# Threshold searches of a capacity router: seven rounds of 17 thresholds, or six of 32

## The chip, the cores and the metric

One core of a Trainium2 chip runs the whole program. The metric is its time on the device in microseconds, from a median of several runs. TensorE (PE) multiplies matrices, VectorE (DVE) and ScalarE (ACT) work on elements, GpSimd (POOL) and SyncE (SP) mostly issue transfers here.

## The reference

The program computes attention (8 batches, 8 heads, 576 positions, heads of 64; half of the heads see a local band, half a stride) and then a mixture of 8 experts over its 4608 tokens. The routing goes through all pairs of token and expert in the order of their logits and gives each expert at most 576 tokens:

```python
cap = N // E
logits = x @ w_gate
order = np.argsort(-logits.flatten())
for idx in order:
    tok, e = (int(idx) // E, int(idx) % E)
    if assigned[tok] >= 0 or counts[e] >= cap:
        continue
    assigned[tok] = e
    counts[e] += 1
for e in range(E):
    mask = assigned == e
    out[mask] = np.maximum(x[mask] @ w1[e], 0.0) @ w2[e]
```

## The kernel before, in words

**Stages.** Until about 226 us the kernel does the attention, writes the tokens to a scratch tensor in DRAM and forms the logits `L` (128 partitions x 36 columns x 8 experts). Then it routes and multiplies expert after expert. "Expert k" is the k-th one that fills up, 0 to 7, which is not its index in the weights. Its FFN is two layers of matmuls (`hidden`, L1150, and the second half of `ffn`, L1169).

**A search (L816).** Which expert fills up next, and at which logit, is found by a search on thresholds. Each token points to its best open expert (`rm` its logit, `ohc` a one-hot row). A round compares all 36 columns of 128 tokens with `J1` thresholds (`cm`, L824, on VectorE), counts the tokens above each threshold per expert on TensorE (L840), folds the counts (`red` L843, `r` L846, a matmul L849), marks the thresholds at which an expert has its 576 tokens (`g`, L856), counts the marks by a matmul (L859) and forms the next, finer thresholds (`cand`, L862). With J1 thresholds a round narrows the interval by J1 + 1. `R1` rounds bring 2^25 steps down to 1 and the last round to 1/16 (L96 to L102). Four of the 36 columns (`GC`) go into one counting matmul, so its stationary operand has GC x J1 columns and a round has 9 of them. Expert 0 has a search of its own (`search0`, 6 rounds of 32 thresholds, L768), and expert 7 takes what is left (`rest`). So there are six searches of this kind.

**After a search.** `number` (L880) gives the expert's index `ei`. `weights` (L978) reads it on SP and loads w1 and w2 (8 transfers of 512 KB) into one buffer each, sums their squares on ScalarE (`jk`, L1002), gets a scale (L1008 to L1011) and cuts each weight into a high and a low fp16 part (`w1h`/`w2h` on ScalarE, L1020; `w1l`/`w2l` on VectorE, L1021), 16 cuts to an expert. `slots` and `indices` (L890, L937) work out which tokens the expert has (`rv` and `ohl` on VectorE, then 36 matmuls, L963), `tokens` (L1066) gathers them with five indirect transfers from POOL and turns them with five transposing transfers from SP (L1075). `close` and `take` strike the expert and its tokens out, and the next search begins.

**What sets the order.** TensorE's order is written by the kernel (ScalarE's too, for expert 0); the other engines' orders come from a scheduler with priorities, where the routing's instructions are marked urgent. The writing is done by a planner at the end of the kernel. It goes through the matmuls of an FFN, adds their nominal time to a `clock`, and steps every chain of side work whose due time has come. A search is such a chain: it waits T_COUNT (2950) before the counting matmuls, T_SUM (1350) before L849 and T_STEP (1225) before L859; in expert 1's search these are multiplied by PACE1 (0.55, L813). Side work itself adds nothing to the clock. Two rules bind the chains to the FFNs: expert ph is numbered only when FFN ph - 2 has been written in full (L1128), and cuts that are not yet written when an expert's FFN begins are written there at once (`rush`, L747 to L751). An FFN's hidden tile is read by ScalarE (`hh`, L1166) and VectorE (`hl`, L1167); three such tiles exist in PSUM.

Of the kernel before, what the change touches and what calls it, by code (L numbers as in the profile page):

```python
# [35 lines left out]
VW = D + 1  # L36
NEG = -8.0e9
BIG = 1.0e30
J1, R1, GC = 17, 7, 4
J0, JL, R0, CUTS0 = 32, 16, 6, (16, 12, 8)  # L40
TP = 128
NC = N // TP
# [1288 lines left out]
```

## Time and profile before

| | |
|---|---|
| three runs | 722.44, 726.11, 727.01 us (median 726.11) |
| the profiled execution | 723.2 us, its span 721.4 us |
| mean granted TensorE clock | 0.893 of full speed |
| attention and logits | to about 226 us |
| expert 0's routing | 226 to about 256 us |
| eight FFNs with the routing of experts 1 to 7 beside them | 256 to about 710 us |
| comparisons of the six searches (L824) | 42, 33.3 us of VectorE |
| DMA traffic | 111 MB, of it 64 transfers of 512 KB for the weights |

In the lines below, a timeline row gives the start in us, the duration in us, engine, source line, operation, and the output tile, an arrow, and its inputs; `x9` merges nine in a row, and the brackets hold the idle time of the engine before it and what ended it. A row by windows gives from:to, the length and, for each engine, busy us with the count of instructions, then the granted clock, the DMA share and GB/s. A row of waits gives total us, times, longest. A row of groups gives busy us and mean ns of one, then the engine's idle time before them.

### The profile page before, as it was taken

To read this page: it belongs to the slowest core of one execution; us is meant where nothing else is said; L and a number is where in the kernel's file an instruction comes from. 1 tells how busy PE (TensorE), PEld (TensorE's weight loads), DVE (VectorE), ACT (ScalarE), POOL (GpSimd) and SP (SyncE) were. 2 spreads that over 40 slices of the span, in tenths; PEclk is the share of its full clock that TensorE was granted. 3 is DMA by queue.
4 is the path that set the end of the run, shared out by engine and by line. 5 is a ranking of instruction groups with operands and counts; after the bars stand their busy time and mean duration, and the time that the engine had idled before them with its cause. 6 is when DMAs were issued, how large, how long until landed. Compare 5 with 4: busy or idle time off the path is not lost.

```text
span 721.4 us, 19211 instructions
## 1 busy us (share of the span) xinstructions
PE 625.3 (87%) x8040; PEld 402.7 (56%) x8043; DVE 455.9 (63%) x1368; ACT 320.8 (44%) x497; POOL 153.7 (21%) x152
## 2 busy tenths in 40 slices
PE   6986978889993479999989998989989998699993
PEld 3664756566663346557537646646644744555741
DVE  4786666786876777867657767757666573662200
ACT  3634634653520156473454364274184265753210
POOL 2053323332330020140040040041041023202011
PEclk9667787985885589999999999999999999899998
DMA  9999999999651360680680491392196079551010
GB/s 248 263 256 221 248 262 260 232 247 214 113 134 50 122 200 1 218 213 2 223 194 15 146 254 33 105 265 63 35 295 103 1 271 262 182 96 52 1 38 29
DMA packets 111401, 111.21 MB, mean 154 GB/s; under 512 B 76332, under 2 KB 84102, under 8 KB 110803
## 3 DMA queue, kind: packets, MB, share of 16 engines
q1 hardware_dynamic: 103235, 88.44, 47.7%
q0 software_dynamic: 7360, 21.15, 9.9%
q8 instruction: 63, 1.03, 0.6%
q10 hardware_dynamic: 720, 0.39, 0.2%
q14 instruction: 23, 0.19, 0.1%
HBM read 73.59 MB, written 18.87 MB: 128 GB/s over the span
## 4 chain that ended last, share of the span: by engine, by line
PE 29%; issue 16%; DVE 7%; DMA 6%; ACT 3%; SPq 3%; POOL 2%; another core or an unknown queue 1%; POOLq 0%; ACTq 0%
PE ph L1159 16%; PE ph L1207 9%; DMA w<-in_w_dram 4%; SPq L1075 2%; DVE w2l L1021 2%; ACT jk L1002 2%; DMA xg<-x_scr,idx 2%; POOL out_dram L1218 1%; DVE w1l L1021 1%; DVE hl L1167 1%; PE ph L1201 1%; POOL xg L1072 1%; SPq L987 1%; PE ph L1060 0%
## 5 line engine op out<-in xcount | busy, mean ns | idle before, releaser
L1159 PE MATMUL ph<-xt,w1h 128*128 128x288 f16 (+2 forms) x1024 | 180.0, 288 | 7.0 <-DMA xt<-xg 4.4
L1218 POOL DMA_INDIRECT out_dram<-y,idx x40 | 43.5, 1087 | 351.3 <-ACT y L1217 324.8
L1159 PEld LDWEIGHTS <-w1h 128*128 128x128 f16 x1024 | 97.1, 98 | 34.5 <-issue 6.7
L1159 PE MATMUL ph<-xt,w1l 128*128 128x288 f16 (+2 forms) x512 | 113.3, 288 | 0.0
L1002 ACT ACTIVATE jk<-w 128x1024 f16<-128x1024 f32 x64 | 67.5, 1055 | 73.2 <-DMA w<-in_w_dram 69.3
L1207 PE MATMUL ph<-w2l,hh 128*128 128x512 f16 x256 | 97.9, 382 | 0.0
L1207 PE MATMUL ph<-w2h,hh 128*128 128x512 f16 x256 | 97.7, 382 | 0.0
L1207 PE MATMUL ph<-w2h,hl 128*128 128x512 f16 x256 | 97.7, 382 | 0.0
L1166 ACT ACTIVATE hh<-ph 128x576 f16<-128x576 f32 (+2 forms) x72 | 42.8, 595 | 120.2 <-PE ph L1159 119.2
L1207 PEld LDWEIGHTS <-hh 128*128 128x128 f16 x512 | 48.7, 98 | 58.0 <-issue 9.5
L1167 DVE SCALAR_TENSOR_TENSOR hl<-ph,hh 128x576 f16<-128x576 f32 (+2 forms) x72 | 49.5, 688 | 43.7 <-ACT hh L1166 43.4
L380 ACT ACTIVATE pr<-spa 128x576 f32<-128x576 f32 x32 | 20.8, 650 | 93.9 <-PE spa L376 89.4
L1159 PEld LDWEIGHTS <-w1l 128*128 128x128 f16 x512 | 49.9, 98 | 12.6 <-issue 0.6
L397 PE MATMUL po<-v_s,pr 64*54 64x65 f32 (+1 forms) x768 | 45.6, 276 | 10.2 <-issue 6.5
L428 POOL TENSOR_TENSOR xos<-xs,xos 118x768 f16<-118x768 f32 x16 | 27.2, 1701 | 119.8 <-ACT xos L427 87.8
L1217 ACT ACTIVATE y<-ph,so 128x512 f32<-128x512 f32 x32 | 21.9, 684 | 67.7 <-PE ph L1207 48.1
L1072 POOL DMA_INDIRECT xg<-x_scr,idx x40 | 40.5, 1012 | 50.2 <-issue 34.7
L1021 DVE SCALAR_TENSOR_TENSOR w1l<-w,w_sw,w1h 128x512 f16<-128x512 f32 x64 | 45.7, 745 | 8.0 <-issue 4.6
L1021 DVE SCALAR_TENSOR_TENSOR w2l<-w,w_sw,w2h 128x512 f16<-128x512 f32 x64 | 45.7, 742 | 7.9 <-ACT y L1217 6.8
L397 PEld LDWEIGHTS po<-v_s,pr 64*54 64x54 f32 (+1 forms) x768 | 34.7, 162 | 17.2 <-issue 11.7
L1207 PEld LDWEIGHTS <-hl 128*128 128x128 f16 x256 | 25.1, 98 | 33.2 <-issue 8.1
L1020 ACT ACTIVATE w1h<-w,w_sw 128x512 f16<-128x512 f32 x64 | 41.8, 710 | 3.9 <-DVE ss_e L203 1.8
(613 smaller groups left out, 961.9 us busy)
## 6 DMA issues: line engine op xcount, KB each, us to landing
w<-in_w_dram SPq DMA_DIRECT2D x64, 512.0 KB
kl<-in_kl_dram SPq DMA_DIRECT2D x16, 304.0 KB
v_s<-in_ns_dram SPq DMA_DIRECT2D x16, 292.5 KB
v_l<-in_nl_dram SPq DMA_DIRECT2D x16, 292.5 KB
ks<-in_ks_dram SPq DMA_DIRECT2D x16, 288.0 KB
qs<-in_qt_dram SPq DMA_DIRECT2D x16, 288.0 KB
ql<-in_qt_dram SPq DMA_DIRECT2D x16, 288.0 KB
x_scr<-xol SPq DMA_DIRECT2D x8, 512.0 KB
```

Source lines behind the costliest of these rows:

```text
L397: nc.tensor.matmul(po[r:r + n, j - j0], pr[k, o:o + n], u.vn[k, t, 2 * p + h], start=(j == j0), stop=(j == j1 - 1), skip_group_check=True)
L428: eng.tensor_tensor(u.xo[:nr, :, 1, c], xf, u.xo[:nr, :, 0, c], op=OP.subtract)
L1002: nc.scalar.activation(jk, wf[:, c * n4:(c + 1) * n4].rearrange("p c f -> p (c f)"), AF.Square, scale=1.41422, accum_out=sq[:, c:c + 1])
L1020: nc.scalar.activation(hi[:, c, f], wf[:, c, f], AF.Copy, scale=s_)
L1021: nc.vector.scalar_tensor_tensor(lo[:, c, f], wf[:, c, f], s_, hi[:, c, f], op0=OP.mult, op1=OP.subtract)
L1072: nc.gpsimd.indirect_dma_start(out=xg[:n], out_offset=None, in_=x_rows, in_offset=bass.IndirectOffsetOnAxis(ap=idx[:n, t:t + 1], axis=0))
L1159: nc.tensor.matmul(tile_[:, j, :w], wt[:, d, f * 128:(f + 1) * 128], xt[:, d // 2, xx, d % 2, c], start=(k == 0), stop=(k == 3 * DC - 1))
L1166: nc.scalar.activation(hv, src, AF.Relu)
L1167: nc.vector.scalar_tensor_tensor(lv, src, 0.0, hv, op0=OP.max, op1=OP.subtract)
L1207: nc.tensor.matmul(py, a[:, f, ts_], w[:, f], start=(k == 0), stop=(k == len(todo) - 1))
L1217: nc.scalar.activation(y, py, AF.Copy, scale=so[:, t:t + 1])
L1218: st = nc.gpsimd.indirect_dma_start(out=out_rows, out_offset=bass.IndirectOffsetOnAxis(ap=idx[:n, t:t + 1], axis=0), in_=y[:n], in_offset= ...
```

## The change

```diff
-J1, R1, GC = 17, 7, 4
+J1, R1, GC = 32, 6, 4
```

A round compares with 32 thresholds and narrows the interval by 33, and there are 6 rounds: the widths go 2^25, 1016802, 30813, 934, 29, 1 and then 1/16. `cm` grows from 36 x 17 = 612 to 36 x 32 = 1152 elements a partition. The stationary operand of the counting matmul grows from 4 x 17 = 68 to 128 columns, the counts in PSUM from 68 to 128 partitions. `fold`, `steps` (R1 x (J1 + 2), 133 to 204 elements), `small` and `cand` (18 to 33 elements) grow with them. Nothing else is edited.

Since the planner steps a search by rounds, each search takes one round less on its clock and all that follows it is written earlier, until the rule on FFN ph - 2 holds it. Three places show this.

On VectorE at the start of FFN 6, the order before has expert 6's last cuts (`w2l`) around expert 7's slots (`inc`, `off`, `slot`, `si`; pr__8903 is expert 7's prefix count):

```order
L1190 TENSOR_SCALAR so<-idx,s_8827 128x5
L1021 SCALAR_TENSOR_TENSOR w2l<-w_8477,w_sw_8483,w2h 128x512 x5
L1167 SCALAR_TENSOR_TENSOR hl<-ph,hh 128x576
L913 SCALAR_TENSOR_TENSOR inc<-ones_f,pr__8903 128x72
L915 TENSOR_TENSOR off<-off,pr__8903 128x72
L1021 SCALAR_TENSOR_TENSOR w2l<-w_8477,w_sw_8483,w2h 128x512
L916 TENSOR_TENSOR off<-off,inc 128x72
L1021 SCALAR_TENSOR_TENSOR w2l<-w_8477,w_sw_8483,w2h 128x512
L918 TENSOR_TENSOR slot<-off 128x36
L1021 SCALAR_TENSOR_TENSOR w2l<-w_8477,w_sw_8483,w2h 128x512
L941 CAST si<-slot 128x36
L1167 SCALAR_TENSOR_TENSOR hl<-ph,hh 128x576
```

The order of the change at the same place (pr__8751 is the prefix count, the tail tile `y` belongs to FFN 5):

```order
L1021 SCALAR_TENSOR_TENSOR w2l<-w_8124,w_sw_8130,w2h 128x512 x3
L1215 SCALAR_TENSOR_TENSOR y<-ph,so,yl 64x512
L1021 SCALAR_TENSOR_TENSOR w2l<-w_8124,w_sw_8130,w2h 128x512 x5
L1008 TENSOR_REDUCE ss<-sq 128x1
L1167 SCALAR_TENSOR_TENSOR hl<-ph,hh 128x576
L913 SCALAR_TENSOR_TENSOR inc<-ones_f,pr__8751 128x72
L915 TENSOR_TENSOR off<-off,pr__8751 128x72
L916 TENSOR_TENSOR off<-off,inc 128x72
L918 TENSOR_TENSOR slot<-off 128x36
L941 CAST si<-slot 128x36
```

The eight cuts have moved into the second layer of FFN 5, and the slots follow one another.

On ScalarE at the same place before, the first sum of squares of expert 7 (`jk` from w_8847) stands between output tiles of FFN 5, ahead of expert 6's w2 cuts (from w_8477):

```order
L1217 ACTIVATE y<-ph,so 128x512
L1002 ACTIVATE jk,sq<-w_8847 128x1024
L1217 ACTIVATE y<-ph,so 128x512
L1020 ACTIVATE w2h<-w_8477,w_sw_8483 128x512 x5
L1166 ACTIVATE hh<-ph 128x576
L1020 ACTIVATE w2h<-w_8477,w_sw_8483 128x512 x3
```

In the change expert 7's squares (from w_8695) stand at the end of FFN 5's first layer, and expert 6's w2 cuts (from w_8124) after them, in its second:

```order
L1166 ACTIVATE hh<-ph 128x576
L1002 ACTIVATE jk,sq<-w_8695 128x1024
L1166 ACTIVATE hh<-ph 128x576
L1002 ACTIVATE jk,sq<-w_8695 128x1024 x3
L1217 ACTIVATE y<-ph,so 128x512
L1020 ACTIVATE w2h<-w_8124,w_sw_8130 128x512 x3
L1214 ACTIVATE yl<-ph,so 64x512
```

The squares have moved ahead by most of an FFN.

On VectorE after expert 4's search, the order before runs through slots, the next search's first comparison (`cm`) and the indices without an FFN instruction between them, because this falls into the second layer of FFN 3:

```order
L935 TENSOR_TENSOR L<-L,pen 128x288
L824 TENSOR_TENSOR cm<-rmn,cand_3712 128x612
L942 TENSOR_SCALAR si<-si 128x36
L943 TENSOR_SCALAR si<-si 128x36
L945 CAST sh<-si 128x72
L947 TENSOR_TENSOR ohh<-sh,iota 128x324
L955 TENSOR_TENSOR ohl_7080<-sh,iota 128x768
L949 TENSOR_TENSOR rv_3713<-ohh,val 128x972
```

In the change the same work falls into the first layer of FFN 3, where every hidden tile has its `hl`:

```order
L935 TENSOR_TENSOR L<-L,pen 128x288
L824 TENSOR_TENSOR cm<-rmn,cand_3712 128x1152
L1167 SCALAR_TENSOR_TENSOR hl<-ph,hh 128x576
L942 TENSOR_SCALAR si<-si 128x36
L943 TENSOR_SCALAR si<-si 128x36
L945 CAST sh<-si 128x72
L947 TENSOR_TENSOR ohh<-sh,iota 128x324
L955 TENSOR_TENSOR ohl_6820<-sh,iota 128x768
L949 TENSOR_TENSOR rv_3713<-ohh,val 128x972
L1167 SCALAR_TENSOR_TENSOR hl<-ph,hh 128x576
```

The `hl` of the running FFN now stand between the comparison, `rv` and the second `ohl`.

## The prediction

> **What bounds the kernel now.** The page's first lines say how much work there is, the stages say who sets the pace. "Expert k" is the k-th expert that is routed, 0 to 7; its FFN is its two layers of matmuls.
>
> ```profile
> span 721.4 us, 19211 instructions
> PE 625.3 (87%) x8040; PEld 402.7 (56%) x8043; DVE 455.9 (63%) x1368; ACT 320.8 (44%) x497; POOL 153.7 (21%) x152
> core 0: us, PE busy (x) PEld busy (x) DVE busy (x) ACT busy (x) POOL busy (x), PEclk, DMA share, GB/s
> 256.00:305.00 49.00, 43.92 (x397) 28.72 (x396) 39.85 (x133) 27.49 (x51) 3.03 (x5) 0.97 0.40 123
> 305.00:360.00 55.00, 54.66 (x434) 33.15 (x435) 38.28 (x121) 27.82 (x46) 10.70 (x10) 1.00 0.49 150
> 592.00:650.00 58.00, 49.79 (x352) 30.50 (x351) 31.21 (x71) 36.76 (x64) 14.20 (x15) 0.94 0.68 180
> ```
>
> Everything that the change touches lies after 256 us. There TensorE is the bound: 54.66 of 55 us busy in a good stretch. VectorE is at 38.28 of 55, so on the average it has room. The routing of a later expert runs beside the FFN of an earlier one, and TensorE takes its instructions in a written order, so a search hurts in two ways: by its own matmuls, and wherever one of them stands at the head of TensorE's queue before VectorE is done. The waits of TensorE from 256 to 650 us, longest first, are the second kind.
>
> ```profile
> PE pr__8971 L963 <- DVE rv L949: 5.4, 1, 5.4
> PE ph L1159 <- DMA xt<-xg: 4.4, 4, 1.6
> PE pr__8005 L849 <- DVE r L846: 3.5, 1, 3.5
> PE pr__5752 L849 <- DVE r L846: 3.2, 1, 3.2
> PE pr__7254 L859 <- DVE g L856: 1.1, 1, 1.1
> PE pr__7185 L1010 <- DVE p L966: 1.1, 1, 1.1
> PE pr__7429 L849 <- DVE r L846: 0.8, 1, 0.8
> PE pr__4649 L840 <- DVE cm L824: 0.4, 1, 0.4
> ```
>
> Of all 42 rounds only one made TensorE wait for its comparison (cm, 0.4 us). So the searches are not waited for directly; their end decides when an expert's tokens and weights come.
>
> **The change part by part.** *Rounds removed.* Six searches (experts 1 to 6) lose one round each. What a round costs TensorE is read from the starts around its three pieces.
>
> ```profile
> 330.06 0.41 PE L1159 MATMUL ph<-xt,w1l 128*128 128x288 f16 x2
> 330.31 0.45 PE L840 MATMUL pr__5247<-ohn,cm 128*68 128x32 f16 x9
> 330.60 0.65 PE L1159 MATMUL ph<-xt,w1h 128*128 128x288 f16 x4
> 331.82 0.29 PE L1159 MATMUL ph<-xt,w1l 128*128 128x288 f16 x1
> 332.04 0.17 PE L849 MATMUL pr__5247<-r,fold 68*17 68x8 f16 x1
> 332.14 0.30 PE L1159 MATMUL ph<-xt,w1l 128*128 128x288 f16 x1
> 333.01 0.53 PE L1159 MATMUL ph<-xt,w1h 128*128 128x288 f16 x3
> 333.48 0.17 PE L859 MATMUL pr__5247<-ih,ones_j 17*128 17x1 f16 x1
> 333.58 0.30 PE L1159 MATMUL ph<-xt,w1h 128*128 128x288 f16 x1
> ```
>
> The nine counting matmuls push the next FFN matmul from 330.31 to 330.60, 0.29 us. Two matmuls of 288 columns started 330.06 and the next thing 330.31, so one takes 0.125: around L849 the distance is 0.32 instead of 0.12, and around L859 (333.01 to 333.58 for three) 0.57 instead of 0.37. A round costs 0.29 + 0.20 + 0.20 = 0.7 us, six of them **-4.2 us**.
>
> *Wider weights.* The 36 rounds left hold 324 counting matmuls, whose stationary operand grows from 68 to 128 columns.
>
> ```profile
> L1159 PEld LDWEIGHTS <-w1h 128*128 128x128 f16 x1024 | 97.1, 98 | 34.5 <-issue 6.7 <-DMA xt<-xg 3.6 <-ACT w1h L1020 0.6
> L840 PEld LDWEIGHTS <-cm 128*68 128x68 f16 x378 | 19.1, 114 | 5.6 <-DVE cm L824 1.5
> 417.92 0.17 PE L1010 MATMUL pr__6434<-ss,ones_b 128*128 128x1 bf16 x1
> 417.95 0.38 PE L1207 MATMUL ph<-w2h,hl 128*128 128x512 f16 x1
> 217.23 1.57 PE L496 MATMUL spb<-wgh,xtl 128*128 128x16 f16 x20 [0.68 <-ACT xtl L489]
> ```
>
> A load of 128 columns lasts 98 ns, one of 68 columns 114. At 417.92 a matmul of one column is followed 0.03 us later by one with 128 fresh columns, so that load fits in 0.03 us, about today's 0.29 / 9 = 0.032. Against it stands L496: twenty matmuls on 128 columns (a few on 64) in 1.57 us, or (1.57 - 0.17) / 19 = 0.074 each. I take **0** for the better likeness to L1010, which stands in the same stream; the other end is 324 x (0.074 - 0.032) = +13.6 us. The Trainium skill, "TensorE: Matmul & The Clock Gate", has both answers: its section "LDWEIGHTS (loading the stationary operand)" makes a load's time its columns over 1.2 ns, an estimate of 50 ns more per load and 16 us in all, which speaks against this change; its section "Weight-path perf modes — Fast Weight Load (FWL) and DoubleRow" has loads of just 128 columns that aren't fp32 go in four chunks at once. The 98 against 114 ns sides with the second.
>
> *Longer comparisons.* cm grows from 612 to 1152 elements a partition.
>
> ```profile
> L824 DVE TENSOR_TENSOR cm<-rmn,cand 128x612 f16<-128x612 f32 x36 | 28.5, 793 | 0.5
> L778 DVE TENSOR_TENSOR cm<-rm,nx 128x512 f16<-128x512 f32 x4 | 2.8, 692 | 0.1
> L778 DVE TENSOR_TENSOR cm<-rm,nx 128x256 f16<-128x256 f32 x4 | 1.7, 419 | 0.0
> L1167 DVE SCALAR_TENSOR_TENSOR hl<-ph,hh 128x576 f16<-128x576 f32 x56 | 42.3, 755 | 41.7 <-ACT hh L1166 41.4
> ```
>
> The comparison of the first search has the same form: (692 - 419) / 256 = 1.07 ns an element, so 1152 take 692 + 640 x 1.07 = 1.37 us, 0.58 more than 0.79. VectorE gets 36 x 1.37 - 42 x 0.79 = +16 us of comparisons, less six times the round's small instructions (about 1 us). In the later searches this lies under the FFN's matmuls: a cm that starts at 328.57 ends before 329.4, and the matmuls that need it start at 330.31, as quoted, so 0.9 us of cover where the need is 0.58. In the first search the planner's distances are multiplied by 0.55 and the cover is gone (the 0.4 us wait is there): 0.58 in each of five remaining rounds after the first is 2.9 at most, none at least; I take four of the five, **+2.3 us**. The wider tables and constants add about 70 elements to two single instructions: nothing.
>
> *Everything after a search moves ahead.* A round is 2950 + 1350 + 1225 = 5525 planner ns (0.55 of it in the first search), and planner ns are matmul time of the FFN. So expert 1's tokens come about 3 us sooner, expert 2's 8, expert 3's 14, expert 4's 19. From expert 5 on the rule that expert ph waits until FFN ph - 2 is written holds it, at the first matmuls of FFN ph - 1. Then three things go.
>
> First, TensorE's wait for transposed tokens (experts 3 and 6): **-4.4 us**, between 0 and 4.4; the lead is far larger than the 1.6 us of the longest. The five gathers and five transposes of each expert move with them, on POOL's queue past two output stores, on SP's past no weight load.
>
> Second, the 5.4 us at FFN 6. Its cause is a block on ScalarE that passes on to VectorE.
>
> ```profile
> 609.54 1.06 ACT L1002 ACTIVATE jk<-w 128x1024 f16<-128x1024 f32 x1 [7.61 <-DMA w<-in_w_dram]
> 611.91 3.40 DVE L1021 SCALAR_TENSOR_TENSOR w2l<-w,w_sw,w2h 128x512 f16<-128x512 f32 x5 [6.78 <-ACT y L1217]
> 619.00:621.00 2.00, 0.00 (x0) 0.50 0.62 172
> 621.00:623.00 2.00, 1.70 (x38) 0.50 0.91 345
> 623.00:625.00 2.00, 2.00 (x11) 0.50 0.86 289
> 625.00:627.00 2.00, 2.00 (x15) 0.83 0.91 291
> ```
>
> ScalarE waited 7.61 us for expert 7's weights, whose load stood on SP behind expert 6's transposes; expert 6's w2 cuts stood behind that and came in front of expert 7's slots and indices on VectorE. The order of the change has these cuts in FFN 5 and expert 7's squares there too. TensorE's clock, granted at 0.50 and 0.83 after the wait, cost it another 0.85 + 1.0 + 0.34 = 2.2 us of busy time. Together **-7.6 us**; the bound is 0, if another wait stands there.
>
> Third, the cuts that are still unwritten when an expert's FFN begins are written there in one heap. With searches that end sooner the heap shrinks, and for experts 5 and 6 it is gone. The waits on g, p and r amid cuts (1.1 + 1.1 + 0.8) are 3.0; **-2 us** of them, between 0 and 3. The two waits of 3.5 and 3.2 us are for VectorE instructions that stood idle though TensorE had delivered, by a releaser that the profile can't name, while tokens were gathered and transposed; the place moves, so I count half, **-3.3 us**, between 0 and -6.7.
>
> *What the move costs.* Numbering, slots and indices of experts 4 and 5, in part 3, now fall into the first layer of an FFN (6 too, with no search behind it), where each of 8 tiles needs an hl of 0.755 us.
>
> ```profile
> 404.00:415.00 11.00, 11.00 (x72) 5.49 (x71) 9.78 (x39) 5.09 (x9) 1.18 (x1) 1.00 0.68 245
> 415.00:426.00 11.00, 11.00 (x100) 5.58 (x99) 7.61 (x27) 10.86 (x20) 6.35 (x6) 1.00 0.86 252
> ```
>
> In the 22 us after expert 3 was numbered VectorE was busy 9.78 + 7.61 = 17.4. Seven more hl (5.3) and three longer cm (1.7) make 24.4: over by 2.4 us, and by the order below they stand ahead of the rv and ohl for which L963 waits. For two and a half experts that is 6 us; L963 had cover of its own, so **+4 us**, between 0 and 2.5 x 7 = 17.5.
>
> The sum: -4.2 + 0 + 2.3 - 4.4 - 7.6 - 2 - 3.3 + 4 = -15.2. The profiled execution took 723.2 us, 1.8 outside its span of 721.4; its span would be 706.2 and its time 708.0. The median of the runs shown is 726.1, 2.9 above the profiled one, so I forecast **711 us**.
>
> **The rivals.** *VectorE becomes the bound of the FFNs (slower).* Each of the 36 comparisons stands in a chain from cand to cm to L840, and if VectorE's queue is full where it runs, the whole 0.58 us shows: +21 us, less 4.2 of rounds, with nothing won, as late hl and rv replace the old waits: 721.4 + 16.8, or 743 against the median. For it speaks 39.85 of 49 us busy in FFN 0 and the 24.4 in 22; against it the cover of 0.9 us and an average of two thirds. It decides once 15 us more of lateness shows than I count, about 0.4 us a round.
>
> *The wide load isn't hidden:* L496's pace, +13.6 us on the forecast: 725, no difference. For it that row, against it L1010 and the load's 98 ns.
>
> *The won waits come back elsewhere:* tokens and weights are early, but the new places collide as often, with code and queues as full as now. Then only rounds and the first search are left, -4.2 + 2.3: 724, no difference. For it speaks that each old wait was a collision of a table of planner times, not a lack of an engine; against it that the tokens' lead grows to many us, and no collision undoes that.
>
> **How the numbers follow.** Forecast 0.72, waits come back 0.12, VectorE the bound 0.10, wide load 0.06. The forecast with the rest of the gains (1.0 + 3.3) and no cost of the move (4) is 711 - 8.3 = 702.7; with the move at 17.5 it is 724.5. The range 702 to 725 leaves out VectorE's case and the outer ends of the others. This kernel's measurement tells about 1% from no change: under 718.8 is faster. The forecast gives nearly all of its chance to that, the two middle rivals almost none, VectorE's case most of its own to slower: faster 0.72, same 0.20, slower 0.08.
>
> **What would show it.** Right: 36 rounds, cm near 1.37 us, L840's nine matmuls still in 0.3 us; no wait on xt; no long wait on rv in FFN 6, ScalarE not blocked on weights there; experts 5's and 6's w2 cuts before their FFN starts; new waits on L963 and L849 in the first layers of FFNs 2 to 4 of some 4 us. Wrong: L840 waiting for cm in most rounds; nine matmuls in over 0.5 us; waits of over 3 us with a halved clock in the first layers; or a PE wait total from 256 to 650 us that isn't at least 10 us under today's.

## The result, and the profile after

The change took 721.88 us (median of 20 runs), the kernel before 726.46 in the same session: a ratio of 0.9928 (95% interval 0.9905 to 0.9951). It is faster, by 4.6 us; 15 were forecast. The interval lies wholly under 1, but the median lies over the 718.8 us under which the prediction spoke of faster. Ratios with an interval leave out executions far above their kernel's fastest (three of the six of rounds_only), and differ from the quotient of the medians by up to 0.5%, in rounds_only by 1.3%. In three later sessions, on chips 5, 9 and 8, the same two kernels gave 0.9883, 0.9931 and 0.9860; two of the three lie outside the first interval, so a session moves this ratio by more than its interval says.

The profiled execution of the change took 713.8 us, its span 712.1. The page's first lines, then the comparison and the weight load by form:

```profile
span 712.1 us, 19031 instructions
PE 614.3 (86%) x7974; PEld 392.3 (55%) x7977; DVE 465.3 (65%) x1326; ACT 318.9 (45%) x497; POOL 156.7 (22%) x152
L824 DVE TENSOR_TENSOR cm<-rmn,cand 128x1152 f16<-128x1152 f32 x30 | 40.6, 1353 | 0.4
L840 PEld LDWEIGHTS <-cm 128*128 128x128 f16 x324 | 12.8, 97 | 9.5 <-DVE cm L824 4.2 <-issue 1.7
```

There are 36 comparisons (30 here, 6 in the other form) of 1.353 us; 1.37 was worked out. A load of 128 columns takes 97 ns where 68 took 114. What nine of them cost TensorE is read from the timeline:

```profile
309.90 0.38 PE L1207 MATMUL ph<-w2h,hl 128*128 128x512 f16 x1
310.11 0.38 PE L840 MATMUL pr__4956<-ohn,cm 128*128 128x32 f16 x9
310.34 0.38 PE L1207 MATMUL ph<-w2h,hh 128*128 128x512 f16 x1
```

From 310.11 to 310.34 is 0.23 us for the nine; before it was 0.29. The wider operand is hidden, and more than that. The waits of TensorE from 256 to 650 us, longest first:

```profile
PE ph L1207 <- DVE w2l L1021: 2.3, 1, 2.3
PE ph L1159 <- ACT xt L1062: 2.0, 1, 2.0
PE ph L1207 <- ACT hh L1166: 1.9, 1, 1.9
PE pr__5641 L849 <- DVE r L846: 1.9, 1, 1.9
PE pr__7713 L849 <- DVE red L843: 1.6, 1, 1.6
PE pr__7012 L849 <- issue: 1.5, 1, 1.5
PE pr__4588 L840 <- DVE cm L824: 1.1, 1, 1.1
PE pr__7585 L963 <- DVE rv L949: 0.9, 1, 0.9
```

The wait on gathered tokens (xt from xg, 4.4) and the 5.4 us on rv in FFN 6 are gone. New are a wait on w2l (2.3, in FFN 0), one on hh (1.9, in FFN 5) and more on cm. The wait on ScalarE's xt (2.0) is not new: before it was 2.5, a row that the list ahead of the result does not show. How the stretches changed is read by windows: FFN 0, FFNs 1 to 4, FFNs 5 and 6, cut at the first matmul of each. First before, then the change (length; then PE busy, and the clock after the five engines):

```profile
260.11:321.32 61.21, 58.81 (x474) 34.98 (x473) 46.27 (x158) 35.00 (x65) 9.76 (x9) 0.97 0.53 155
321.32:551.78 230.46, 217.35 (x1726) 131.77 (x1725) 152.32 (x487) 109.67 (x180) 43.07 (x40) 0.99 0.48 136
551.78:662.93 111.15, 102.74 (x756) 62.77 (x755) 62.86 (x182) 59.07 (x98) 20.42 (x20) 0.97 0.48 140
```

```profile
259.19:324.21 65.02, 59.19 (x471) 34.45 (x471) 51.23 (x157) 35.19 (x65) 10.85 (x9) 0.95 0.52 146
324.21:551.88 227.67, 217.81 (x1705) 128.89 (x1704) 172.93 (x519) 113.20 (x188) 44.57 (x40) 0.99 0.48 140
551.88:653.57 101.69, 98.81 (x709) 60.89 (x708) 46.93 (x112) 53.99 (x90) 20.35 (x20) 1.00 0.50 148
```

FFN 0 is 3.8 us longer, FFNs 1 to 4 are 2.8 us shorter, FFNs 5 and 6 9.5; FFN 7 is the same in all kernels (47.2). Length less PE busy is TensorE's idle time: 2.4, 13.1 and 8.4 us before, 5.8, 9.9 and 2.9 in the change.

### The profile page after: what moved, and what is told of

Same layout as the page of the kernel before. It is cut to its first block, busy times and chain, and to the rows that moved or that the text cites. A ratio compares the mean times of both kernels' runs of the same rounds, so it can differ in the third digit from the quotient of the medians.

```text
span 712.1 us, 19031 instructions
## 1 busy us (share of the span) xinstructions
PE 614.3 (86%) x7974; PEld 392.3 (55%) x7977; DVE 465.3 (65%) x1326; ACT 318.9 (45%) x497; POOL 156.7 (22%) x152
## 4 chain that ended last, share of the span: by engine, by line
PE 26%; issue 12%; DVE 10%; DMA 8%; ACT 3%; POOL 2%; SPq 1%; POOLq 0%; ACTq 0%
PE ph L1207 12%; PE ph L1159 8%; DMA w<-in_w_dram 7%; PE ph L1201 2%; DVE w2l L1021 2%; ACT jk L1002 2%; DVE cm L824 1%; POOL out_dram L1218 1%; DVE hl L1167 1%; SPq L987 1%; DVE w1l L1021 1%; DMA xg<-x_scr,idx 1%; POOL xg L1072 1%; ACT hh L1166 1%; DVE ohl L955 1%
## 5 line engine op out<-in xcount | busy, mean ns | idle before, releaser
L1159 PE MATMUL ph<-xt,w1h 128*128 128x288 f16 (+2 forms) x1024 | 177.5, 287 | 2.0 <-ACT xt L1062 2.0
L1159 PE MATMUL ph<-xt,w1l 128*128 128x288 f16 (+2 forms) x512 | 111.4, 287 | 0.0
L1072 POOL DMA_INDIRECT xg<-x_scr,idx x40 | 43.2, 1080 | 135.5 <-DVE idx L975 100.5
L397 PE MATMUL po<-v_s,pr 64*54 64x65 f32 (+1 forms) x768 | 41.3, 259 | 5.3 <-issue 3.8
L1020 ACT ACTIVATE w2h<-w,w_sw 128x512 f16<-128x512 f32 x64 | 41.0, 710 | 5.0 <-DVE w_sw L208 4.9
```

The lines of the kernel that those rows point to most:

```text
L397: nc.tensor.matmul(po[r:r + n, j - j0], pr[k, o:o + n], u.vn[k, t, 2 * p + h], start=(j == j0), stop=(j == j1 - 1), skip_group_check=True)
L1020: nc.scalar.activation(hi[:, c, f], wf[:, c, f], AF.Copy, scale=s_)
L1072: nc.gpsimd.indirect_dma_start(out=xg[:n], out_offset=None, in_=x_rows, in_offset=bass.IndirectOffsetOnAxis(ap=idx[:n, t:t + 1], axis=0))
L1159: nc.tensor.matmul(tile_[:, j, :w], wt[:, d, f * 128:(f + 1) * 128], xt[:, d // 2, xx, d % 2, c], start=(k == 0), stop=(k == 3 * DC - 1))
```

## The experiments

The table has every run. A difference is between medians, against the kernel before in the same session; the interval is that of the ratio. The last three columns are from each run's one profile, cut as above; that of hybrid_17 is left out, as it shows an execution of 725.75 us, 3.8 over the median. Diffs are shortened: the three planner waits stand in one line with others (L48).

| kernel | median us, difference | ratio (95%) | FFN 0 | FFNs 1-4 | FFNs 5-6 |
|---|---|---|---|---|---|
| before, two profiles | - | - | 61.2, 60.9 | 230.5, 230.1 | 111.2, 111.5 |
| change | 721.88, -4.6 | 0.9905-0.9951 | 65.0 | 227.7 | 101.7 |
| again | 715.59, -8.8 | 0.9842-0.9925 | 65.1 | 222.9 | 103.0 |
| move_only | 714.99, -9.4 | 0.9838-0.9909 | 62.8 | 228.1 | 100.5 |
| rounds_only | 716.82, -7.6 | 0.9708-0.9820 | 59.5 | 221.2 | 112.0 |
| wide_only | 725.23, +0.8 | 0.9984-1.0055 | 64.0 | 223.9 | 114.0 |
| slow_first | 716.29, -9.1 | 0.9797-0.9910 | 65.2 | 225.0 | 104.0 |
| early_first | 713.23, -12.2 | 0.9792-0.9864 | 62.8 | 217.4 | 110.9 |
| again_2 | 718.65, -6.7 | 0.9888-0.9973 | 64.7 | 223.5 | 102.3 |
| hybrid | 712.64, -13.2 | 0.9780-0.9896 | 64.9 | 218.1 | 107.6 |
| hybrid_17 | 721.91, -3.9 | 0.9880-0.9967 | | | |
| hybrid_slow | 714.47, -11.3 | 0.9833-0.9933 | 62.2 | 223.1 | 108.3 |
| rounds_again | 719.91, -5.9 | 0.9810-0.9968 | 62.7 | 220.8 | 112.7 |
| early_cut6 | 715.97, -6.9 | 0.9902-0.9973 | 65.2 | 216.6 | 112.8 |
| hybrid_cut6 | 715.32, -7.6 | 0.9883-0.9955 | 64.7 | 216.3 | 111.0 |
| lift | 707.58, -15.3 | 0.9796-0.9873 | 64.8 | 217.4 | 104.6 |
| before_cut6 | 727.08, +4.2 | 1.0010-1.0092 | 61.1 | 228.9 | 116.7 |
| lift_again | 708.73, -14.7 | 0.9766-0.9868 | 64.8 | 216.4 | 107.7 |
| again_3 | 711.43, -12.0 | 0.9806-0.9914 | 65.1 | 223.9 | 102.4 |

### The change taken apart: rounds, width, place

**again**: the change, unedited.

> The change once more, for a profile of a more typical execution: the one shown took 713.84 us where the median of twenty is 721.88. Expected a ratio of 0.990 to 0.996. Theory A (the move of the work wins, part of it is lost to a late VectorE in FFNs 0 and 1 and in the first layers of FFNs 3 and 4): the wait on xt and the long wait on rv in FFN 6 are absent in this profile too, and what it takes more than 712.1 us of span lies in FFNs 0 to 4. Theory B (waits come back elsewhere, only the rounds count): a wait of 3 us or more with a lowered clock stands in some FFN, at another place than in the first profile.

**move_only**: against the kernel before,

```diff
-T_COUNT, T_SUM, T_STEP = 2950, 1350, 1225
+T_COUNT, T_SUM, T_STEP = 2529, 1157, 1050
-X1 = 100
+X1 = 86
```

> Seven rounds of 17 as before, but the planner's three waits of a round are shortened by 6/7 (2529, 1157 and 1050, and the first step's margin with them), so that each search ends on the planner's clock where it ends in the change. No round saved, no longer comparison. Theory A: at least the change's own gain, 0.985 to 0.993, with no wait on xt and no wait of over 3 us on rv in FFN 6. Theory B: the move is worth nothing, 0.998 to 1.002, with other waits in place of those. In FFN 0 the rounds stand closer, so if hurry is what costs there, FFN 0 is longer than the 61.2 us of before here as well (65.0 in the change's profile).

**rounds_only**: against the change,

```diff
-T_COUNT, T_SUM, T_STEP = 2950, 1350, 1225
+T_COUNT, T_SUM, T_STEP = 3442, 1575, 1429
-X1 = 100
+X1 = 117
```

> Six rounds of 32 as in the change, but the planner's three waits of a round are lengthened by 7/6 (3442, 1575 and 1429), so that each search ends where it ended before. Rounds saved and longer comparisons, no move. Theory A: six rounds of 0.7 us less, FFN 0 unhurried, the old waits on xt and in FFN 6 still there: -2 to -4 us, 0.994 to 0.998. Theory B: all of the change's gain, 0.991 to 0.994.

**wide_only**: against the kernel before,

```diff
-J1, R1, GC = 17, 7, 4
+J1, R1, GC = 32, 7, 4
```

> Seven rounds of 32: the order and the planner's clock of before, only the comparison, the weights and the folds are the wide ones of the change. The price of the width by itself. Theory A: 1 to 3 us in the first search and nothing behind it, 1.001 to 1.005, L840's nine matmuls still in 0.3 to 0.4 us. If the wide load is not hidden: 378 x 0.042 = 16 us, 1.022. If every comparison's 0.58 us shows: 42 x 0.58 = 24 us, 1.034.

The change repeated (again) gave 0.9883, under the 0.990 to 0.996 that were expected. Width by itself gave 1.002, no price that can be told from none, so both rivals that made it dear (1.022 and 1.034) fall. In wide_only's profile FFN 0 is 3 us longer, as expected, and TensorE waits more for tokens, but FFNs 1 to 4 are 6.4 us shorter: the two waits of 3.5 and 3.2 us for a VectorE that stood idle, which the profile before has there, are absent. Its waits on tokens and on rv:

```profile
PE ph L1159 <- DMA xt<-xg: 10.3, 8, 2.2
PE pr__8971 L963 <- DVE rv L949: 2.4, 1, 2.4
```

The move alone brings -9.4 us and the rounds alone -7.6, and the change, which has both, -8.8 in the same session. They don't add up. The -7.6 is the least certain of the three: the six times of rounds_only lie in two groups, 706 to 711 and 722 to 730 us. Theory A, which gave the rounds 2 to 4 us and the move the rest, is wrong on the rounds; theory B is wrong on the move. The table shows where they overlap: rounds_only has the shortest FFN 0 and keeps its 112 us in FFNs 5 and 6, the change gives 5 us in FFN 0 and 2 or more in FFNs 1 to 4 and gets 9 back at the end.

### The first search

**slow_first**: against the change, the first search's pace as long as before.

```diff
-PACE1 = 0.55
+PACE1 = 0.64
```

> The change with the first search unhurried: its factor is 0.64 in place of 0.55, so that expert 1's search ends on the planner's clock where it ended before (6 x 0.64 is 7 x 0.55); the other searches keep the change's distances. Theory C (in FFN 0 the longer comparisons, in a hurried search, make VectorE late with expert 0's w2l, and the second layer waits 2.3 us and then runs 1 us long on a lowered clock): FFN 0 falls from 65.0 to about 60 us, no wait on w2l, and the kernel is 4 to 6 us faster than the change, a ratio of 0.980 to 0.985 where the change has 0.988. Theory B (a wait that goes here comes back elsewhere): the same ratio as the change, within 0.003.

**early_first**: against the change, the first search as in the change, the others late.

```diff
-T_COUNT, T_SUM, T_STEP = 2950, 1350, 1225
+T_COUNT, T_SUM, T_STEP = 3442, 1575, 1429
-PACE1 = 0.55
+PACE1 = 0.4714
```

> The other half: the first search as hurried as in the change, the searches of experts 2 to 6 with the distances lengthened by 7/6. Theory C: FFN 0 at 64 to 65 us with the wait on w2l; the tokens of the later experts come about as late as before, less 3 us, so waits on xt of 2 to 5 us and the block on rv in FFN 6 are back: 4 to 8 us more than the change, a ratio of 0.993 to 1.0. If hurry in FFN 0 costs nothing, it equals the run with rounds saved and no move, 0.989.

**again_2** and **before_again** are the change and the kernel before, unedited.

> The change a third time: its ratio was 0.9928 and then 0.9883. Expected 0.987 to 0.994; its profile shows FFN 0 at 64 to 66 us with a wait on w2l of 2 us or more, and the eight FFNs together at 438 to 442 us. If one of the stalls of 2 to 3.5 us on L849 is in it, at a place where the two profiles so far have none, these stalls come with the execution and not with the place in the program.

> The kernel before, unedited, for a second profile. The one shown has two stalls on r at L849 of 3.5 and 3.2 us and 450.0 us for the eight FFNs. If the stalls come with the execution: absent here or at other places, and the FFNs at 443 to 447 us. If they belong to the place: both are here again. The waits on xt and the wait on rv in FFN 6 should be here in either case.

Theory C missed in both runs. Its wait on w2l does not come from the longer comparison by itself. In the change expert 0's last w2l stands on VectorE behind expert 1's indices (`ohl`), 8 us after ScalarE has finished the w2h that it reads. Here are ScalarE, VectorE and TensorE in the change:

```profile
289.72 1.32 ACT L1020 ACTIVATE w2h<-w,w_sw 128x512 f16<-128x512 f32 x2
298.57 1.01 DVE L955 TENSOR_TENSOR ohl<-sh,iota 128x768 f16<-128x768 f16 x2
299.50 0.73 DVE L1021 SCALAR_TENSOR_TENSOR w2l<-w,w_sw,w2h 128x512 f16<-128x512 f32 x1
300.29 0.50 PE L1207 MATMUL ph<-w2l,hh 128*128 128x512 f16 x1 [2.28 <-DVE w2l L1021]
```

In all ten profiles with this wait the last w2l stands there; in move_only, whose searches end at the same places, it comes at 294.73, ahead of the indices, and TensorE does not wait for it. What puts it last in the scheduler's order is not shown.

In slow_first the wait on w2l is gone, and the ratio, 0.9853, comes near to what was expected, but FFN 0 stays at 65.2 us: VectorE stood for 3.27 us before a red whose counts had long been there, and TensorE with it. Here is that place on VectorE, then on TensorE:

```profile
313.88 0.19 DVE L843 TENSOR_TENSOR red<-pr__4974,fold 128x32 f16<-128x32 f32 x1 [3.27 <-remote]
```

```profile
311.36 0.38 PE L1207 MATMUL ph<-w2h,hl 128*128 128x512 f16 x1
314.90 0.17 PE L849 MATMUL pr__4974<-r,fold 128*32 128x8 f16 x1 [3.16 <-DVE r L846]
315.00 0.61 PE L1207 MATMUL ph<-w2h,hh 128*128 128x512 f16 x1
```

And early_first, expected to be worse than the change, is better: 0.983 against 0.993 in one session, the intervals apart. Its waits on gathered tokens (xt from xg) are down to 0.3 us, though only expert 1's search is shortened; 3 us of lead on the planner's clock are enough. Its three stretches:

```profile
263.29:326.12 62.83, 56.63 (x462) 32.94 (x462) 50.14 (x153) 35.05 (x65) 10.81 (x9) 1.00 0.54 152
326.12:543.56 217.44, 214.25 (x1682) 129.07 (x1680) 158.57 (x460) 108.47 (x180) 44.11 (x40) 1.00 0.50 144
543.56:654.45 110.89, 101.47 (x743) 62.10 (x742) 62.80 (x175) 58.99 (x98) 20.60 (x20) 0.97 0.48 141
```

FFNs 1 to 4 take 217.4 us, 5 to 10 less than in the change's four profiles, with 3.2 us of idle; FFNs 5 and 6 take 110.9, with 9.4 idle. Part of this is only moved work: the change has 1705 matmuls in FFNs 1 to 4 where this has 1682, and 709 against 743 in FFNs 5 and 6. In before_again the waits on xt and rv are at their places, and so is the stall before the same red of FFN 4:

```profile
542.90 0.19 DVE L843 TENSOR_TENSOR red<-pr__8005,fold 68x32 f16<-68x32 f32 x1 [2.84 <-remote]
```

The other one, in FFN 1, is smaller: TensorE waits 1.9 us there where it waited 3.2. again_2 has no wait over 1.4 us at L849. The stall of FFN 4 is in both profiles of this kernel, so it seems to come with the place and not with the execution.

### Where the searches should end

**hybrid**: early_first, and in `pace`

```diff
-        return t if len(closed) > 1 else t * PACE1
+        return t * PACE1 if len(closed) == 1 else t * 6 / 7 if len(closed) > 4 else t
```

> Six rounds of 32, the first search hurried as in the change, the searches of experts 2 to 4 at the distances lengthened by 7/6 (so these experts come where they came before, less 3 us of the planner's clock), those of experts 5 and 6 at the change's distances, so that expert 6 is numbered 14 us earlier than before. Theory D (3 us of lead remove the waits on xt; every further us of lead pushes slots and indices into the first layers of the FFNs and costs there; only expert 6 needs the lead, for the block in FFN 6): FFNs 1 to 5 at 269 to 273 us together as in the run with the early first search (269.0; the change's profiles have 276.9), the first layer of FFN 6 at 25 to 28 us in place of 35.5, ratio 0.965 to 0.975. Theory B (what goes here comes back elsewhere): 0.980 to 0.986, the same as with the early first search alone.

**hybrid_17**: the kernel before with the same `pace` and PACE1 = 0.4714, so that its seven rounds of 17 end where the hybrid's six end.

> The same places on the planner's clock as in the hybrid, but with seven rounds of 17 as before. It tells what the rounds themselves bring once the places are good. By the sum on record the hybrid's rounds are worth 4.2 us less the first search's 2.3: this run 2 to 5 us over the hybrid. If the longer comparisons eat what the rounds save: the same as the hybrid or up to 3 us under it. With the measured pair of places before (seven rounds of 32 against six: 8 us of the median) it would be more than 5 over.

**hybrid_slow**: the hybrid with PACE1 = 0.51. **rounds_again**: rounds_only, unedited.

> The hybrid with the first search a little less hurried (its factor 0.51 in place of 0.4714; expert 1 numbered at 21.2 us of the planner's clock in place of 19.7 in the change and 23.0 before). Theory D: tokens still 1.5 us ahead of before, the wait on w2l in FFN 0 smaller than 2.3 us or gone: FFN 0 at 60 to 62 us, ratio 0.961 to 0.975, up to 3 us under the hybrid. Theory B: another stall of 2 to 3 us stands in FFN 0 in its place, as when the first search was unhurried.

> The rounds saved with no move, a second time: its six times fell into two groups, 706 to 711 and 722 to 730 us, and its ratio was read from the lower group alone. If the place is a knife edge (a wait on xt or in FFN 6 that comes or not), both groups are here again, in one session. Otherwise one group of 712 to 720 us, a ratio of 0.985 to 0.992.

The hybrid keeps FFNs 1 to 4 at 218.1 us, as theory D said, but FFN 6 still has its block (32.9 us, a wait on rv of 6.9), and the ratio stays at 0.984. At equal places the six rounds of 32 are worth 9.3 us of the median over seven of 17 (712.64 against 721.91), and some 6 us by the ratios (0.9838 against 0.9923); both are more than the 4.2 on record. hybrid_slow loses the wait on w2l and wins 2.7 us in FFN 0, but 5 go elsewhere; it is no better. rounds_again spreads as widely as rounds_only did (709.9 to 731.2 us), but its six times show no two groups. What makes this kernel's times spread isn't shown, since the profiles hold shorter executions only.

### The block in FFN 6

The chain in the hybrid's first layer of FFN 6 (it begins at 595.8 us): SP's weight loads and SP's wait between them, then ScalarE, then VectorE, then TensorE.

```profile
583.30 18.87 SPq L987 DMA_DIRECT2D w<-in_w_dram  x8
```

```profile
SPq L987 <- DVE w2l L1021: 14.0, 1, 14.0
```

```profile
603.72 1.06 ACT L1002 ACTIVATE jk<-w 128x1024 f16<-128x1024 f32 x1 [4.51 <-DMA w<-in_w_dram]
...
606.96 0.63 ACT L1166 ACTIVATE hh<-ph 128x576 f16<-128x576 f32 x1
```

```profile
607.62 0.76 DVE L1167 SCALAR_TENSOR_TENSOR hl<-ph,hh 128x576 f16<-128x576 f32 x1 [8.21 <-ACT hh L1166]
608.30 0.29 DVE L913 TENSOR_TENSOR_SCAN inc<-ones_f,pr__8753 128x72 f32<-128x72 f32 x1
```

```profile
611.59 0.56 PE L963 MATMUL pr__8821<-ohl,rv 128*32 128x64 f16 x12 [6.88 <-DVE rv L949]
```

Expert 7's weights wait on SP for expert 6's cuts to free the buffers, ScalarE's square jk waits for them, hh stands behind it, hl behind hh, and the slots behind hl. The head of the chain is not the same in every kernel: before, the loads stand behind expert 6's transposes, as the prediction read it (596.01 to 605.47 us, the loads from 605.72). Four runs try to break the chain.

**early_cut6** is early_first with

```diff
-                yield step if ph else min(step, T_BULK0)
+                yield step * 0.6 if ph == 6 else step if ph else min(step, T_BULK0)
```

> The run with only the first search early (0.983), and one line more: expert 6's squares and cuts follow one another at 0.6 of the planner's distances, so that all are written before FFN 6 begins. Nothing else moves. Theory D (the block in FFN 6 comes from expert 6's w2 cuts that are still unwritten when FFN 6 begins; they hold expert 7's weights, these hold ScalarE's squares, and behind those stand hh, hl and rv): the wait on rv (6.9 us) is gone or under 2 us, the first layer of FFN 6 at 25 to 28 us in place of 35.5, FFN 5 at most 4 us longer, ratio 0.968 to 0.976. Theory B: what goes in FFN 6 comes back in FFN 5, ratio 0.981 to 0.986.

**hybrid_cut6** is the hybrid with 0.85 there, **before_cut6** the kernel before with 0.55.

> The hybrid (0.984), whose expert 6 is numbered 4.5 us of the planner's clock too late for its cuts to be written before FFN 6, with these at 0.85 of their distances, which is just enough. Theory D: first layer of FFN 6 at 25 to 28 us in place of 32.9, ratio 0.970 to 0.978. Theory B: 0.982 to 0.986.

> The kernel before, seven rounds of 17, with expert 6's squares and cuts at 0.55 of their distances: the block in FFN 6 by itself, which the sum on record put at 7.6 us. Theory D: the first layer of FFN 6 at 26 to 29 us in place of 33.9 and 34.8 (the waits on xt there may stay), the wait on rv gone, 5 to 8 us less in all, ratio 0.989 to 0.994. Theory B: 0.997 to 1.002.

**lift** is early_first with another `pace`:

```diff
-        return t if len(closed) > 1 else t * PACE1
+        return t * PACE1 if len(closed) == 1 else t * 0.825 if len(closed) > 3 else t
```

> No change of the cuts' distances: the searches of experts 4, 5 and 6 run at 0.825 of the lengthened distances (expert 4 numbered at 155.5 us of the planner's clock, 5 at 197, 6 at 238.7; in the change 145, 190 and 236), so that expert 6's cuts end before FFN 6 by its earlier numbering alone. Theory D: FFN 6 at 25 to 27 us, FFNs 1 to 3 as with the early first search (162.8 in all), FFNs 4 and 5 between its 106.0 and the change's 110 to 111; ratio 0.972 to 0.980.

Writing the cuts closer does not help. The FFNs of early_cut6 and hybrid_cut6 take 441.7 and 439.2 us in their profiles, where early_first and hybrid, in other sessions, took 438.4 and 437.8; before_cut6 is slower than before (1.005). Its rv wait went from 5.4 to 0.4 us, but another came in FFN 5, since the sum of expert 6's squares was now asked for before its weights had landed:

```profile
PE pr__8583 L1010 <- DVE ss L1008: 4.9, 1, 4.9
PE ph L1159 <- DMA xt<-xg: 4.0, 2, 2.5
```

So theory D's cause, cuts that are unwritten when FFN 6 begins, is not enough; for this edit theory B is right. What does sort the runs is when SP has issued the last of expert 7's loads, against the start of FFN 6 (start plus duration of the SP row, and the first matmul of the layer):

| kernel | last load after FFN 6's start, us | FFN 6, first layer, us |
|---|---|---|
| again, again_3, slow_first, again_2 | -7.8, -6.9, -6.9, -6.4 | 25.2, 25.2, 25.2, 25.2 |
| change | -4.5 | 25.7 |
| move_only | -2.6 | 27.2 |
| lift, lift_again | +1.1, +1.3 | 31.6, 33.3 |
| early_cut6, hybrid_cut6 | +2.5, +2.9 | 31.7, 35.0 |
| before_cut6, hybrid | +5.2, +6.4 | 30.7, 32.9 |
| hybrid_slow, hybrid_17 | +7.9, +8.2 | 33.0, 33.2 |
| rounds_again | +14.2 | 32.6 |
| wide_only, before, before_again | +15.3, +15.4, +16.5 | 34.1, 33.9, 34.8 |
| rounds_only, early_first | +16.2, +17.7 | 35.5, 35.5 |

Loads issued before FFN 6 starts: 25 to 27 us. After: 31 to 36, however late. This sorts the runs; no run moved the loads alone, so it is not shown as the cause. The closer cuts did bring the loads forward, by 15 us from early_first to early_cut6 and by 10 from before to before_cut6, but not past the start of FFN 6. There the loads stand on SP behind expert 6's transposes (in early_cut6 589.73 to 599.06 us, the loads from 599.32), and these wait for its tokens. Only the kernels in which every search from expert 2's on is shorter on the planner's clock (the change, move_only, slow_first) have the loads out before that start. In the lift the wait on rv is gone and one on a PSUM tile that ScalarE empties late has come:

```profile
PE ph L1159 <- ACT y L1217: 4.5, 1, 4.5
```

So the first layer of FFN 6 took 31.6 us where 25 to 27 were expected. The lift is at 707.6 us, and -15.3 is the most of all medians; FFNs 1 to 4 stay at 217 us. By its ratio (0.9835) it is level with early_first (0.9828) and hybrid (0.9838) in their sessions.

**lift_again** and **again_3** put it beside the change.

> The lift (first search early, experts 2 and 3 about where they were before, 4 to 6 lifted so that expert 6's cuts end before FFN 6) beside the change in one session: the lift was 0.9835 in a session without the change. Theory D: 0.976 to 0.987 again, FFN 0 at 64 to 65.5 us, FFNs 1 to 4 at 216 to 219 us, FFNs 5 and 6 at 103 to 106 us, and at least 4 us under the change in the median. If it was the session: within 3 us of the change.

> The change a fourth time, in the lift's session: ratio 0.987 to 0.994. Profile: FFN 0 at 64.5 to 65.5 us, FFNs 1 to 4 at 222 to 228, FFNs 5 and 6 at 101 to 104.

In one session the lift has 708.73 and the change 711.43 us, with ratios of 0.9817 (0.9766 to 0.9868) and 0.9860 (0.9806 to 0.9914). The profiles keep their order (FFNs 0 to 7 at 434.0 and 436.1 us against 437.7 to 441.6 in four of the change), but by time the two aren't told apart here: the 4 us expected are 2.7, which by the words on record is the session's case. FFNs 5 and 6 of lift_again, 107.7 us, are over the 103 to 106 expected.

## Why the prediction was right or wrong

The change is faster, as forecast, but by 4.6 us of the median and not by 15. Three steps of the prediction failed. The first is the last one of the sum: the distance from the profiled execution to the median was carried over as 2.9 us and was 8.0. The second is the first search, put at +2.3: FFN 0 grew by 3.9 us where the sum gives 1.6. The third is that the gains in FFNs 5 and 6 (the -7.6 and most of the -4.4) were counted whole, with no new wait: one on hh, in two profiles with a lowered clock behind it, gave back about 2 us. Why the median lies so far over the profile stays open.

The forecast was 711 us and the result 721.9, a miss of 10.9. Of it 5.1 lie between the profiled execution and the median, and 5.8 in the profiled execution (713.8 where 708.0 was worked out): 2.3 in FFN 0, 3.1 in FFNs 1 to 4, 1.5 in FFNs 5 and 6, less 1 outside the FFNs. The change's other profiles came nearer. In the mean the eight FFNs shrank from 449.9 us (two profiles before) to 439.0 (four of the change), by 10.9 where the sum has 15.2. The terms below are held against these means.

- **Rounds, -4.2: mis-sized.** At equal places and width one round less in each search is 8.4 us of the median (725.23 for wide_only, 716.82 for rounds_only), 6.7 with rounds_again of another session in its place. In the profiles of the first pair TensorE's busy time in the FFNs fell by 3.5 us (426.2 to 422.7), about the 4.2 of the sum; its idle time fell by 5.8 (22.9 to 17.1), and that the sum put at nothing. A likely reason, not tested, is that a round's whole chain through VectorE ends sooner too. This gain is not added to that of the move: the two alone are 9.4 and 7.6, together 8.8.
- **Wider weights, 0: right.** 0.23 us for nine matmuls and 1.002 in wide_only; the rival of 13.6 us falls. This agrees with the Trainium skill, "TensorE: Matmul & The Clock Gate", section "Weight-path perf modes — Fast Weight Load (FWL) and DoubleRow", and not with the columns over 1.2 ns of the section "LDWEIGHTS (loading the stationary operand)": the trace has 97 ns for 128 columns and 114 for 68.
- **First search, +2.3: too small, and mostly another mechanism.** With expert 1's round (-0.7) FFN 0 should have grown by 1.6 us; it grew by 3.9 (61.1 to 65.0). The cm waits came as said (1.1 and 0.7 us), but the first layer, where they are, grew by 0.6 only. Not foreseen was the second layer: expert 0's last w2l stands behind expert 1's indices, TensorE waits 2.3 us for it, and in all four profiles of the change the clock fell after that.
- **xt, -4.4: right.** None is left, in four profiles. But 3 us of lead on the planner's clock nearly do it (0.3 us are left in early_first); the 8 to 19 us on record weren't needed.
- **FFN 6, -7.6 with the clock: mechanism right, gain partly given back.** With the xt waits there (2.8) and expert 6's round (0.7), 11.1 us were to go from FFNs 5 and 6; 9.0 went. FFN 5 has a new wait on hh of 1.9 to 2.7 us, and in two profiles the lower clock behind it.
- **Stalls, -3.3, and heaps, -2; cost of the move, +4.** With xt in FFN 3 (1.6) and four rounds (2.8), FFNs 1 to 4 were to shrink by 5.7 us; they shrank by 5.8 in the mean, but by 2.6 in the change's first profile and by 6.4 to 7.4 in the others, so that the sum came out is partly luck. TensorE's idle time in the second layers of FFNs 1 and 4, where the stalls were, fell from 7.6 us (6.2 in before_again) to 1.3 to 3.4, by more than the 3.3 counted. The new waits in the first layers of FFNs 2 to 4 are there: idle of 3.0 (again) to 5.5 us (change) against 2.6 before, of which 1.6 were xt.
- **From the profile to the median, +2.9: wrong.** The change's profiled execution is 8.0 us under its median, in the other sessions 6.3, 8.2 and 2.7, and in all four runs it is the shortest of its run; for the kernel before the distance was 2.9 and 1.1. A longer execution tends to have a lower mean clock (again: 0.908 at 709.3 us, 0.885 at 718.9). But only one execution of a run has a trace, so what lengthens the others stays open.

One sign of being wrong that was on record, waits of TensorE from 256 to 650 us that are not at least 10 us under before's, is there in the change's profile: they fell by about 6 (26.4 to 20.6), because FFN 0 and FFN 5 got new ones. In the later profiles the totals are 14.4, 18.3 and 15.6, so in two of the four the sign is absent. Of the rivals, VectorE as the bound and the wide load are out. "The won waits come back elsewhere" is right in part: for FFN 0's hurry (w2l, then the stall), for the cuts of expert 6, and for the clock; it is wrong for xt and for most of FFN 6. Its time, 724, is nearer to the result than the forecast's 711; it takes the profiles to tell the two apart.

## What to carry to other kernels

Price a shorter chain and an earlier place as one thing when both take away the same wait: here each alone brought 6 to 9 us, and both together 9 in the same session. An earlier place wins until the wait is covered, here for the tokens with 3 us of lead; with more lead FFNs 1 to 4 were 5 to 10 us longer, so move each item by what its own consumer needs. And when a wait ends a chain over several queues, look for the transfer at its head: closing up the middle moved the waits and did not shorten the FFNs as a whole.

## What the runs showed of the hardware

A wait of about 2 us is enough to lower TensorE's clock, though not always. After the wait on w2l in FFN 0 the change's second profile (again) has, in stretches of 2 us,

```profile
300.00:302.00 2.00, 2.00 (x44) 1.39 (x42) 0.64 (x3) 0.60 (x1) 1.03 (x1) 0.54 0.68 226
302.00:304.00 2.00, 2.00 (x14) 0.75 (x10) 0.34 (x2) 0.00 (x0) 0.75 (x1) 0.61 0.83 299
304.00:306.00 2.00, 2.00 (x14) 0.81 (x14) 1.10 (x7) 1.24 (x2) 1.39 (x3) 1.00 0.76 216
```

that is 0.92 + 0.78 = 1.7 us lost, while early_first with the same wait of 2.28 us runs on at 1.00. Nine of ten profiles with this wait show the drop. The length of the wait does not decide it: in FFN 5 a lower clock followed waits on hh of 2.00 us (again) and 2.08 us (again_3), but not those of 1.91 us (change) and 2.67 us (again_2).

VectorE's stalls of about 3 us with no releaser that the profile can name (3.27 us in slow_first, 2.84 in before_again) stand where an expert's tokens are being gathered or transposed. The two that the kernel before shows are not in wide_only, which has the same places on the planner's clock. The cause of these stalls was not found.
